# Block order of a two-layer SSM and SwiGLU kernel: the second layer's block 0 taken third instead of fourth

## Chip, core and metric

The kernel runs on one core of a Trainium2 chip. The metric is device time in microseconds (us) of one execution. Before the change the median of three runs is 1167.27 us (1165.26 to 1168.05).

## What is computed

The input is a sequence of 2048 rows (time) by 512 columns (channels), float32. Two layers follow each other, with the same weights; each is an SSM part and an FFN part, both on the layer-normed input and with the input added back:

```
x = x + A(layernorm(x)); x = x + B(layernorm(x)); x = x + A(layernorm(x)); x = x + B(layernorm(x))
A: K = Re(sum_n C exp(dt A l) dt B)   # a filter of 2048 taps per channel, from 128 states
   y = irfft(rfft(u padded) * rfft(K padded))[:2048] + u * Dskip
B: (silu(x @ w_gate) * (x @ w_up)) @ w_down      # 512 -> 1376 -> 512
```

A is a causal convolution along the sequence. B works on each row alone.

## The kernel before

**Blocks.** The sequence is cut into NB = 4 blocks of T = 512 rows. A pair (l, b) names layer l and block b; (l, b) has an SSM block and an FFN block, eight pairs in all. SEQ (line 45) is the order in which they are taken. The first some 320 us of the kernel build the filter's spectra and split the weights into high and low float16 halves; then the eight pairs follow.

**SSM block** (`inputs`, `forward`, `ssm`, `ssm_half`). For each pair not prepared early, `inputs` (line 709) loads 512 rows (tile `n`, from the program's input in layer 0, from `xdr` in layer 1), normalises them (`norm_x`: row statistics on ACT, the power on POOL, L226 on DVE, L249 on ACT), and `forward` makes eight *steps*, one for each column half h and frequency part q. A step's forward transform is DVE work (bt, z, the low half of z, all L230) and 12 matmuls (L282, tile `pf`), copied by ACT to `u`, which POOL stores in `udr`. `ssm_half` then multiplies spectra on DVE: block b needs b + 1 products (L778) and b sums (L781) of 128x1024 a step, since it convolves with all earlier blocks of its layer, whose `u` and filter parts it loads over SP's queue (`uu`, `w`). So a step of block 0 has one such large operation, block 1 three, block 2 five, block 3 seven. L783 and L784 combine, the result is split in two (`yl`), 12 matmuls (L798, tile `pi`) transform back, and `combine` adds up (`bb`). After four steps some 14 DVE operations of 128x256 (L813 to L830, and L230 under `t1`, `t2`, `xf`, `xg`) add the half into `xt`. `ahead` holds inputs made one step before their use: the last step of a block already makes the first input of the next.

**FFN block** (`ffn`, `ffn_norm`). It works on two halves of 256 rows. `ffn_norm` takes row statistics on ACT, splits the normed rows into two float16 tiles (`nn`, on DVE L864) and transposes them by DMA over SP's queue into `mix`. Then come six groups of matmuls into `pgu`: five of 48 (L911, L912, L914) and a *remainder* of 48 small ones (L878 to L880) that stands first in its half; after each group ACT takes silu (L917), DVE multiplies (L918), ACT and DVE split (L919, L920). The down projection `py` (L926 to L928) is 66 matmuls of 512 columns, after each 33 of which DVE adds the residual (L931) and SP stores the rows to `xdr` (layer 0) or to the output. The last L931 of an FFN block marks its end.

**Dependences.** SSM block (0, b) reads the program's input and earlier blocks of its layer. SSM block (1, b) reads the output of FFN block (0, b) and the spectra of earlier blocks of layer 1. An FFN block reads its own SSM block.

**Order.** The loop at the end of the kernel writes the SSM block of the pair i + 1 and then the FFN block of the pair i. From there on a list scheduler places instructions on each engine's queue by priorities: FFN evacuations and norms and the transform matmuls are high, the rest goes by the place in the program. On the chip each engine works through its queue in that fixed order. Tiles come from pools with few buffers (`n` 1, `u` 2, `w` and `uu` 3), and `xs` rotates over three blocks by the index in SEQ. HALF and INV (both 2) say from which index in SEQ the transforms use float16 halves; they are indices, so the third pair is the first of that kind under both orders.

Of the kernel before, what the change touches and what calls it, by code (L numbers as in the profile page):

```python
# [41 lines left out]
HALF = 2  # L42
INV = 2
LOW = [a for a in range(1, 33) if a % 2] + [8, 16, 24, 32]
SEQ = ((0, 0), (0, 1), (0, 2), (1, 0), (0, 3), (1, 1), (1, 2), (1, 3))


def dft_constants():
# [26 lines left out]
def kernel(ctx, tc, x, a_re, a_im, b_re, b_im, c_re, c_im, log_dt, d_skip,  # L75
# [12 lines left out]
    def tl(shape, name, tag, dt=F32):  # L88
        return sb.tile(shape, dt, name=name, tag=tag, bufs=BUFS[tag])
# [4 lines left out]
    def psml(shape, name):  # L94
        return ps.tile(shape, F32, name=name, tag="sml", bufs=4)
# [133 lines left out]
    def stt(o, i0, s, i1, op1):  # L229
        V.scalar_tensor_tensor(o, i0, s, i1, OP.mult, op1)  # L230

    def load_x(xt, layer, b):
        if layer == 0:
            nc.sync.dma_start(xt, x[0, b * T:(b + 1) * T, :].rearrange("(c p) d -> p c d", p=P))
        else:
            nc.sync.dma_start(xt, xdr[b].rearrange("c p d -> p c d"))
# [5 lines left out]
    def whole(t):  # L242

        return t.rearrange("p i (c d) -> p i c d", c=NQ)

    def norm_x(n):
        rs, nb = row_stats(n, 4, 1.0, "stats", lambda r: tl([P, D], "junk", "t1", BF16))
        for c in range(4):
            A.activation(n[:, c], n[:, c], AF.Identity, scale=rs[:, c:c + 1], bias=nb[:, c:c + 1])  # L249
# [454 lines left out]
    def inputs():  # L704

        for layer, b in SEQ:
            if layer == 0 and b < 2:
                if b == 0:
                    nc.sync.dma_start(u4, udr[0][0, 0].rearrange("q p c i d -> p q c i d"))
                for h in range(2):  # L710
                    for i, q in enumerate(QORD):
                        if b == 0:
                            u = u4[:, q]
                            for qn in (QORD[:3], QORD[3:], (), ())[i] if h else ():
                                nc.sync.dma_start(u4[:, qn], udr[0][0, 1, qn])
                        else:
                            u = tl([P, NQ, 2, DC], "u", "u")
                            nc.sync.dma_start(u, udr[0][b, h, q])
                        yield h, q, u
                continue  # L720
            n = tl([P, 4, D], "n", "n")
            load_x(n, layer, b)
            norm_x(n)
            if (layer, b) == SEQ[HALF]:
                eh.append(tl([P, 4, 3, 2, P], "eh", "ef", F16))
                nc.sync.dma_start(eh[0], c_eh)
            for h in range(2):
                for q, u in forward(n, h, eh[0] if eh else None):
                    if b < NB - 1:
                        G.dma_start(udr[layer][b, h, q], u)  # L730
                    yield h, q, u

    def ssm(layer, b):

        if (layer, b) == SEQ[INV]:
            nc.sync.dma_start(eih, c_eih)
        for h in range(2):
            yield from ssm_half(layer, b, h)

    def ssm_half(layer, b, h):  # L740
        first = layer == 0 and b == 0
        half = SEQ.index((layer, b)) >= INV
        hs = slice(h * HD, (h + 1) * HD)
        bb = {}

        def combine(q, pi):
            if q < 2:
                pair = tl([P, 2, 2, HD], "bb", "bd") if h == 0 or not first else bb1[:, q]
                bb[q], bb[q, 1] = pair[:, 0], pair[:, 1]
                A.activation(bb[q], pi, AF.Copy, scale=sy[:, 1:2] if half else 1.0)  # L750
                return
            s = bb[3 - q]
            bb[q] = bb[3 - q, 1]
            if half:
                stt(bb[q], pi, sy[:, 2:3], s, OP.add)
                stt(s, pi, sy[:, 1:2], s, OP.add)
            else:
                V.tensor_tensor(bb[q], s, pi, OP.subtract)
                V.tensor_tensor(s, s, pi, OP.add)

        late = []
        for _ in range(4):
            hq, q, u = ahead.pop(0)
            nxt = next(spec, None)
            if nxt:
                ahead.append(nxt)
            yk = tl([P, NQ, 2, 2, DC], "yk", "y1")
            y = yc if half else tl([P, 2, HD], "yf", "w")
            for k in range(b + 1):
                if k == 0:  # L770
                    w, uu = w0r[:, h, q], u
                else:
                    w = tl([P, NQ, 2, DC], "w", "w")
                    nc.sync.dma_start(w, wdr[k, h, q])
                    uu = tl([P, NQ, 2, DC], "uu", "uu")
                    nc.sync.dma_start(uu, udr[layer][b - k, h, q])
                t = tl([P, NQ, 2, 2, DC], "t", "t") if k else yk
                V.tensor_tensor(t, uu.unsqueeze(2).to_broadcast([P, NQ, 2, 2, DC]),  # L778
                                w.unsqueeze(3).to_broadcast([P, NQ, 2, 2, DC]), OP.mult)
                if k:  # L780
                    V.tensor_tensor(yk, yk, t, OP.add)  # L781
            yo = whole(y)
            V.tensor_tensor(yo[:, 0], yk[:, :, 0, 0], yk[:, :, 1, 1], OP.subtract)  # L783
            V.tensor_tensor(yo[:, 1], yk[:, :, 0, 1], yk[:, :, 1, 0], OP.add)  # L784
            if half:
                yl = yl2[:, QORD.index(q) % 2]
                A.activation(yl[:, 0], y, AF.Copy, scale=sy[:, 0:1])
                stt(yl[:, 1], y, sy[:, 0:1], yl[:, 0], OP.subtract)
            pi = psml([P, 2, HD], "pi")
            with tc.high_priority(offset=0 if first else BOOST):  # L790
                for o in range(2):
                    if half:
                        terms = [(eih[:, q, 0 if i == o else 1 + o, le], yl[:, ly, i])
                                 for i in range(2) for le, ly in ((0, 0), (0, 1), (1, 0))]
                    else:
                        terms = [(ei[:, q, 0 if i == o else 1 + o], y[:, i]) for i in range(2)]
                    for k, (e, m) in enumerate(terms):
                        PE.matmul(pi[:, o], lhsT=e, rhs=m, start=k == 0, stop=k == len(terms) - 1)  # L798
            late.append((q, pi))
            if first and q < 2 or len(late) > 1:  # L800
                combine(*late.pop(-1 if first and q < 2 else 0))
            yield
        for l in late:
            combine(*l)
        s03, e03, d03, f03 = bb[0][:, 0], bb[0][:, 1], bb[3][:, 0], bb[3][:, 1]
        s12, e12, d12, f12 = bb[1][:, 0], bb[1][:, 1], bb[2][:, 0], bb[2][:, 1]
        xt = xs[SEQ.index((layer, b)) % 3]
        if h == 0 and not first:
            load_x(xt, layer, b)
        o = [xt[:, c, hs] for c in range(4)]  # L810
        t1 = tl([P, HD], "t1", "t1")
        t2 = tl([P, HD], "t2", "t1")
        V.tensor_tensor(t1, s03, s12, OP.add)  # L813
        stt(t2, d12, TT, e12, OP.subtract)
        V.tensor_tensor(o[0], o[0], t1, OP.add)
        stt(t1, e03, -TT, d03, OP.add)
        V.tensor_tensor(t1, t1, t2, OP.add)
        stt(o[1], t1, CC, o[1], OP.add)
        yield
        t1 = tl([P, HD], "t1", "t1")  # L820
        t2 = tl([P, HD], "t2", "t1")
        V.tensor_tensor(s03, s03, s12, OP.subtract)
        V.tensor_tensor(f03, f03, f12, OP.add)
        stt(t2, d03, TT, e03, OP.subtract)
        stt(t1, e12, TT, d12, OP.subtract)
        V.tensor_tensor(s03, s03, f03, OP.subtract)
        V.tensor_tensor(t1, t1, t2, OP.add)
        stt(o[2], s03, HH, o[2], OP.add)
        stt(o[3], t1, CC, o[3], OP.add)
        yield  # L830
# [22 lines left out]
    def ffn_norm(layer, b, s):  # L853

        rows = TB // P
        xt = xs[SEQ.index((layer, b)) % 3][:, s * rows:(s + 1) * rows]
        nh, nlo = nhl2[:, s % 2, 0], nhl2[:, s % 2, 1]
# [95 lines left out]
    with tc.manual_schedule(engines={mybir.EngineType.Activation, mybir.EngineType.DVE, mybir.EngineType.PE, mybir.EngineType.Pool}):  # L953
# [167 lines left out]
        spec, ahead = inputs(), []  # L1121
# [27 lines left out]
        load_x(xs[0], 0, 0)  # L1149
        split(0, 0, 3)  # L1150
        conv = [ssm_half(0, 0, h) for h in range(2)]

        def slots():
# [115 lines left out]
```

## Time and profile before

| | |
|---|---|
| median of three runs | 1167.27 us |
| profiled execution, its own time | 1163.83 us |
| its span, first to last instruction | 1161.1 us |
| mean granted TensorE clock | 0.989 |
| PE busy (weight loads) | 95% (76%) |
| DVE, ACT, POOL busy | 86%, 52%, 9% |
| 9942 matmuls, 1586 DVE instructions | |

PE is TensorE's matmuls and PEld its weight loads, which run beside them; DVE is VectorE, ACT ScalarE, POOL GpSimd, SP the queue that issues most DMAs. A busy share is of the span. Matmuls overlap in the pipeline, so the duration of one is longer than the distance between two starts. In a row of the timeline stand start and duration in us, engine, line, operation, output and input by the program's names, the count, and in brackets the idle time before it and who ended it. All times are of the one profiled execution.

### The profile page before, as it was taken

What the parts mean: (1) busy time and instruction counts of PE and PEld (TensorE: products, weight loads), DVE (VectorE), ACT (ScalarE), POOL (GpSimd) and SP (SyncE); (2) the same over time, 40 slices, a digit from 0 to 9 for tenths busy, and PEclk for the clock granted to TensorE, in tenths of its full rate; (3) what the DMA queues carried; (4) which work ended last, traced back from release to release, by engine and by line L of the source; (5) the groups of instructions that cost most, each with busy time, mean ns of one, the idle gap of its engine ahead of it and who ended that gap; (6) DMA issues with size and microseconds to landing.
All of it is one profiled execution on the core that took longest, in us unless ns stands there. A gap on an engine that the chain in (4) does not pass through costs nothing.

```text
span 1161.1 us, 24400 instructions
## 1 busy us (share of the span) xinstructions
PE 1101.9 (95%) x9942; PEld 877.3 (76%) x9942; DVE 998.6 (86%) x1586; ACT 599.7 (52%) x1198; POOL 109.7 (9%) x162
## 2 busy tenths in 40 slices
PE   2989999998889999999999999999999999999998
PEld 1868888886776868687868687868777686876875
DVE  7999999968789999999899999989994999983212
ACT  6889898733553463557453533655433452334211
POOL 1112222210000010010010000210000010000000
PEclk9989999998899999999999999999999999999999
DMA  5357677866394437332264444343534145312000
GB/s 208 129 162 164 161 178 175 187 172 226 112 289 119 145 119 222 105 111 74 79 155 134 127 161 145 103 132 88 164 109 150 49 121 158 102 42 46 15 23 19
DMA packets 127314, 150.38 MB, mean 130 GB/s; under 512 B 50897, under 2 KB 75985, under 8 KB 127202
## 3 DMA queue, kind: packets, MB, share of 16 engines
q1 hardware_dynamic: 115298, 123.32, 34.9%
q0 software_dynamic: 11904, 25.50, 9.5%
q8 instruction: 78, 1.28, 0.5%
q14 instruction: 34, 0.28, 0.1%
HBM read 98.70 MB, written 33.82 MB: 114 GB/s over the span
## 4 chain that ended last, share of the span: by engine, by line
DVE 30%; PE 30%; issue 7%; DMA 4%; ACT 3%; SPq 1%; POOL 1%; DVEq 0%; ACTq 0%; POOLq 0%
PE pgu L911 5%; PE pgu L912 5%; PE pgu L914 5%; DVE t L778 5%; DVE yk L781 4%; PE py L926 3%; PE py L927 3%; PE py L928 3%; DVE yk L778 3%; DVE z L230 3%; DVE sg L918 2%; PE pi L798 2%; PE pf L282 2%; DVE hl L920 2%; DMA w<-wdr 2%
## 5 line engine op out<-in xcount | busy, mean ns | idle before, releaser
L911 PE MATMUL pgu<-mix,wsl 128*128 128x256 f16 x1280 | 299.2, 273 | 5.5 <-DVE sg L918 5.0
L912 PE MATMUL pgu<-mix,wsl 128*128 128x256 f16 x1280 | 298.9, 273 | 0.0
L914 PE MATMUL pgu<-mix,wsl 128*128 128x256 f16 x1280 | 195.2, 273 | 0.0
L912 PEld LDWEIGHTS <-wsl 128*128 128x128 f16 x1280 | 125.2, 98 | 22.7 <-issue 6.4
L926 PE MATMUL py<-wsl,hh 128*128 128x512 f16 (+1 forms) x352 | 133.5, 379 | 4.9 <-DVE xg L931 3.0
L911 PEld LDWEIGHTS <-wsl 128*128 128x128 f16 x1280 | 125.1, 98 | 16.4
L914 PEld LDWEIGHTS <-wsl 128*128 128x128 f16 x1280 | 125.2, 98 | 15.3
L928 PE MATMUL py<-wsl,hl 128*128 128x512 f16 (+1 forms) x352 | 133.4, 379 | 0.5 <-DVE hl L920 0.5
L927 PE MATMUL py<-wsl,hh 128*128 128x512 f16 x320 | 121.3, 379 | 0.0
L778 DVE TENSOR_TENSOR t<-uu,w 128x1024 f32<-128x1024 f32 x96 | 116.9, 1218 | 3.5 <-DMA w<-wdr 3.2
L917 ACT ACTIVATE sg<-pgu,sc 128x512 f32<-128x512 f32 x80 | 54.6, 683 | 125.1 <-PE pgu L914 121.8
L781 DVE TENSOR_TENSOR yk<-yk,t 128x1024 f32<-128x1024 f32 x96 | 116.8, 1217 | 0.2
L918 DVE SCALAR_TENSOR_TENSOR sg<-pgu,sc,sg 128x512 f32<-128x512 f32 x80 | 59.6, 745 | 52.1 <-ACT sg L917 51.9
L533 PE MATMUL pw<-kt,ek 128*128 128x256 f32 (+1 forms) x384 | 92.2, 378 | 0.0
L919 ACT ACTIVATE hh<-sg 128x512 f16<-128x512 f32 x80 | 50.1, 627 | 79.5 <-DVE sg L918 79.5
L533 PEld LDWEIGHTS pw<-kt,ek 128*128 128x128 f32 x384 | 73.6, 196 | 8.6
L798 PE MATMUL pi<-yl,mix 128*128 128x256 f16 x576 | 78.9, 273 | 0.6 <-DVE yl L230 0.3
L282 PE MATMUL pf<-z,eh 128*128 128x256 f16 x576 | 74.9, 273 | 0.6 <-DVE z L230 0.6
L778 DVE TENSOR_TENSOR yk<-u,w0r 128x1024 f32<-128x1024 f32 x56 | 68.1, 1217 | 0.8 <-ACT u L284 0.8
L498 PE MATMUL pk<-re,g 128*32 128x64 f32 x1024 | 65.1, 317 | 3.6 <-DMA g<-g 1.9
L920 DVE TENSOR_TENSOR hl<-sg,hh 128x512 f16<-128x512 f32 x80 | 54.9, 686 | 15.5 <-ACT hh L919 15.4
L927 PEld LDWEIGHTS <-hh 128*128 128x128 f16 (+1 forms) x352 | 34.4, 98 | 41.6 <-issue 6.0
(237 smaller groups left out, 2165.9 us busy)
## 6 DMA issues: line engine op xcount, KB each, us to landing
w<-wdr SPq DMA_DIRECT2D x96, 256.0 KB, 2.7
uu<-udr SPq DMA_DIRECT2D x96, 256.0 KB, 3.0
udr<-u POOLq DMA_DIRECT2D x32, 256.0 KB, 2.6
g<-g POOLq DMA_DIRECT2D x6, 1024.0 KB, 9.1
udr<-u SPq DMA_DIRECT2D x16, 256.0 KB, 3.0
n<-xdr SPq DMA_DIRECT2D x4, 1024.0 KB, 5.7
kdr<-ks SPq DMA_DIRECT2D x6, 512.0 KB, 2.6
kt<-kdr SPq DMA_DIRECT2D x24, 128.0 KB, 2.9
```

What stands on the lines that cost most here:

```text
L282: PE.matmul(pf[:, o], lhsT=e, rhs=m, start=k == 0, stop=k == len(terms) - 1)
L533: PE.matmul(pw[:, i], lhsT=e, rhs=kt[:, :, c + 4 * k0:4 * k1:4, :].rearrange("p g k d -> p k g d"), start=c == 0, stop=c == 3)
L778: V.tensor_tensor(t, uu.unsqueeze(2).to_broadcast([P, NQ, 2, 2, DC]), w.unsqueeze(3).to_broadcast([P, NQ, 2, 2, DC]), OP.mult)
L781: V.tensor_tensor(yk, yk, t, OP.add)
L798: PE.matmul(pi[:, o], lhsT=e, rhs=m, start=k == 0, stop=k == len(terms) - 1)
L911: PE.matmul(o, lhsT=wgu(wi, k, 0)[:, fs], rhs=nh[:, k], start=k == 0, stop=False)
L912: PE.matmul(o, lhsT=wgu(wi, k, 1)[:, fs], rhs=nh[:, k], start=False, stop=False)
L914: PE.matmul(o, lhsT=wgu(wi, k, 0)[:, fs], rhs=nlo[:, k], start=False, stop=k == 3)
L918: V.scalar_tensor_tensor(sg, pgu[:, 1], sc6[:, 4:5], sg, OP.mult, OP.mult)
L926: PE.matmul(py[:, r], lhsT=hh[:n, f, rc], rhs=wd(f, 0)[:n], start=f == 0, stop=False)
L927: PE.matmul(py[:, r], lhsT=hh[:n, f, rc], rhs=wd(f, 1)[:n], start=False, stop=False)
L928: PE.matmul(py[:, r], lhsT=hl[:n, f, rc], rhs=wd(f, 0)[:n], start=False, stop=f == FT - 1)
```

## The change

Two entries of SEQ change places, so that (1, 0) is taken third and (0, 2) fourth. FFN block (0, 0), on which SSM block (1, 0) depends, is written after SSM block (0, 1); so the early input of the third pair can no longer be made in the last step of SSM block (0, 1), and the second part of the diff leaves it out there (nxt is None at that one step) and makes it at the first step of the third pair.

```diff
-SEQ = ((0, 0), (0, 1), (0, 2), (1, 0), (0, 3), (1, 1), (1, 2), (1, 3))
+SEQ = ((0, 0), (0, 1), (1, 0), (0, 2), (0, 3), (1, 1), (1, 2), (1, 3))
...
         late = []
-        for _ in range(4):
+        for s in range(4):
+            if not ahead:
+                ahead.append(next(spec))
             hq, q, u = ahead.pop(0)
-            nxt = next(spec, None)
+            nxt = None if (layer, b, h, s) == (*SEQ[1], 1, 3) else next(spec, None)
             if nxt:
                 ahead.append(nxt)
```

Lines behind line 762 have numbers that are higher by two in the changed kernel (L778 is L780 there, L918 L920, L920 L922, L931 L933, L864 L866).

The queues change at these places. The first is DVE in the second half of FFN block (0, 0). Before the change, from that half's fourth group (L918) on; the products are those of the first two steps of SSM block (0, 2), bt is its forward transform:

```order
L918 SCALAR_TENSOR_TENSOR sg_3072<-pgu,sc_92,sg_3072 128x512
L783 TENSOR_TENSOR mix<-yk 128x256
L784 TENSOR_TENSOR mix<-yk 128x256
L778 TENSOR_TENSOR t<-uu,w 128x1024
L230 SCALAR_TENSOR_TENSOR xg<-t_3318,xg 128x256
L230 SCALAR_TENSOR_TENSOR t_3326<-bb 128x256
L629 TENSOR_SCALAR sy<-sy 128x1
L230 SCALAR_TENSOR_TENSOR bt<-n 128x256 x6
L778 TENSOR_TENSOR yk<-u,w0r 128x1024
```

With the change, from the third group on (the nn splits are those of FFN block (0, 1)):

```order
L920 SCALAR_TENSOR_TENSOR sg_3072<-pgu,sc_92,sg_3072 128x512
L866 TENSOR_TENSOR nn_3036<-nn_3036 128x512
L922 TENSOR_TENSOR hl<-sg_3072,hh 128x512
L866 TENSOR_TENSOR nn_3036<-nn_3036 128x512
L920 SCALAR_TENSOR_TENSOR sg_3072<-pgu,sc_92,sg_3072 128x512
L922 TENSOR_TENSOR hl<-sg_3072,hh 128x512
L226 SCALAR_TENSOR_TENSOR rs<-mv,rs 128x2
L920 SCALAR_TENSOR_TENSOR sg_3072<-pgu,sc_92,sg_3072 128x512
```

The products and transforms of SSM block (0, 2) have left the place; FFN operations and the norms of the next FFN block are what is left. The first forward operation of SSM block (1, 0) (bt) stands behind the fourth group of FFN block (0, 1).

The second place is DVE behind the last residual add of FFN block (0, 1). Before the change (the add, L931, is the first row; bt and z are those of SSM block (0, 3), L918 is FFN block (0, 2)'s second group):

```order
L931 SCALAR_TENSOR_TENSOR xg<-py,sc_92,xg 128x512
L230 SCALAR_TENSOR_TENSOR bt<-n 128x256 x4
L230 SCALAR_TENSOR_TENSOR z_3073<-bt 128x256 x2
L230 SCALAR_TENSOR_TENSOR z_3073<-z_3073 128x2x256
L230 SCALAR_TENSOR_TENSOR z_3073<-bt 128x256 x2
L918 SCALAR_TENSOR_TENSOR sg_3072<-pgu,sc_92,sg_3072 128x512
```

With the change 15 instructions stand between that add and the first of these rows, which end with the second nn split of the next FFN block, (1, 0); `xf` is the block's `xt`, and the products (L780, L783) are those of the second and third step of SSM block (0, 2):

```order
L780 TENSOR_TENSOR t_5484<-uu_5482,w_5480 128x1024
L230 SCALAR_TENSOR_TENSOR xf_3075<-t1_4558,xf_3075 128x256
L226 SCALAR_TENSOR_TENSOR rs_5918<-mv_5917,rs_5918 128x2
L783 TENSOR_TENSOR yk_5471<-yk_5471,t_5484 128x1024
L785 TENSOR_TENSOR mix_2445<-yk_5471 128x256
L786 TENSOR_TENSOR mix_2445<-yk_5471 128x256
L780 TENSOR_TENSOR t_5532<-uu_5530,w_5528 128x1024
L866 TENSOR_TENSOR nn2_3036<-nn2_3036 128x512
L780 TENSOR_TENSOR yk_5526<-u_5468,w0r_91 128x1024
L230 SCALAR_TENSOR_TENSOR yl2_3074<-mix_2445,sy_94,yl2_3074 128x512
L783 TENSOR_TENSOR yk_5526<-yk_5526,t_5532 128x1024
L866 TENSOR_TENSOR nn2_3036<-nn2_3036 128x512
```

The norm of the next FFN block stood well ahead of that add before; now it stands 27 instructions behind it. Behind the last residual add of FFN block (0, 2) the changed queue reads in the same way, with 32 instructions up to the second nn split of FFN block (0, 3).

## Prediction

> **What bounds the kernel now.** I read the kernel by stages first: one window for each of the eight FFN blocks, cut where the last residual add of a block (L931) starts on DVE. Columns: stretch, its length, busy time (and count) of PE, PE's weight loads, DVE, ACT, POOL, then the granted clock, DMA share, GB/s.
>
> ```profile
> 340.00:440.00 100.00, 97.90 (x788) 73.42 (x787) 96.48 (x166) 44.96 (x90) 8.87 (x11) 1.00 0.46 134
> 440.00:559.00 119.00, 117.35 (x1002) 92.29 (x1000) 114.28 (x210) 68.00 (x137) 11.91 (x18) 1.00 0.38 120
> 559.00:666.00 107.00, 105.19 (x890) 81.42 (x888) 103.70 (x165) 47.96 (x94) 6.29 (x5) 1.00 0.47 131
> 666.00:776.00 110.00, 109.40 (x930) 85.39 (x929) 107.35 (x184) 56.39 (x109) 11.72 (x13) 1.00 0.42 128
> 776.00:881.00 105.00, 104.23 (x884) 80.86 (x883) 102.05 (x162) 43.17 (x79) 7.03 (x12) 1.00 0.43 130
> 881.00:979.00 98.00, 97.44 (x821) 74.69 (x820) 80.40 (x128) 44.62 (x90) 6.36 (x5) 1.00 0.40 114
> 979.00:1075.00 96.00, 95.65 (x807) 73.25 (x805) 69.40 (x109) 33.01 (x61) 1.80 (x4) 1.00 0.24 70
> 1075.00:1161.00 86.00, 81.28 (x644) 59.89 (x641) 18.22 (x26) 13.95 (x22) 0.20 (x1) 0.99 0.06 19
> ```
>
> From 440 on PE never rests: between 440 and 1075 its idle time is 1.7 + 1.8 + 0.6 + 0.8 + 0.6 + 0.3 = 5.8 us. DVE is as full until 881 and then empties. So the end is PE's amount of work plus the time in which PE has nothing ready. The change moves work and takes none away; it can gain at most those 5.8 us and loses each microsecond in which PE starves. PE is fed because the next FFN block's input is ready early:
>
> ```profile
> 520.47 0.15 DVE L226 SCALAR_TENSOR_TENSOR rs<-mv,rs 128x2 f32<-128x2 f32 x1
> 558.04 0.75 DVE L931 SCALAR_TENSOR_TENSOR xg<-py,sc,xg 128x512 f32<-128x512 f32 x1
> ```
>
> At 520 the normalisation of FFN block (0,2) has its scale; the add that ends FFN block (0,1) comes at 558. The stock is over 30 us. The question is whether it survives.
>
> **What the change does to the stock.** SSM block (1,0) now stands third, and its input is the output of FFN block (0,0). While PE does that FFN, DVE, which in the old order worked on SSM block (0,2), has only FFN operations. The trace shows what such a dependence costs, since SSM block (1,3) waits for FFN block (0,3):
>
> ```profile
> 438.28 0.74 DVE L931 SCALAR_TENSOR_TENSOR xg<-py,sc,xg 128x512 f32<-128x512 f32 x1
> ...
> 879.59 0.75 DVE L931 SCALAR_TENSOR_TENSOR xg<-py,sc,xg 128x512 f32<-128x512 f32 x1
> ...
> 901.60 2.14 DVE L230 SCALAR_TENSOR_TENSOR bt<-n 128x256 f32<-128x256 f32 x6 [1.42 <-ACT n L249]
> ...
> 1106.84 0.75 DVE L931 SCALAR_TENSOR_TENSOR xg<-py,sc,xg 128x512 f32<-128x512 f32 x1 [4.50 <-PE py L928]
> ...
> 1149.04 0.75 DVE L931 SCALAR_TENSOR_TENSOR xg<-py,sc,xg 128x512 f32<-128x512 f32 x1 [4.21 <-PE py L928]
> ```
>
> From the add to the first forward operation (bt) pass 22.0 us: store, load, row statistics on ACT. Two adds of successive half blocks, with PE alone at work, are 42.2 us apart: an FFN half is 42.2 us of PE, a block 84.4. The matmuls of the transforms come from the chain of waits, the DVE prices from the groups (last numbers: busy us, mean ns):
>
> ```profile
> 437.39 1.31 PE pf L282 x12
> ```
> ```profile
> L778 DVE TENSOR_TENSOR t<-uu,w 128x1024 f32<-128x1024 f32 x96 | 116.9, 1218 | 3.5 <-DMA w<-wdr 3.2
> L781 DVE TENSOR_TENSOR yk<-yk,t 128x1024 f32<-128x1024 f32 x96 | 116.8, 1217 | 0.2
> L230 DVE SCALAR_TENSOR_TENSOR z<-bt 128x256 f32<-128x256 f32 x96 | 36.3, 417 | 0.1
> L230 DVE SCALAR_TENSOR_TENSOR bb<-pi,sy,bb 128x512 f32<-128x512 f32 x48 | 35.7, 744 | 4.3 <-PE pi L798 4.2
> L864 DVE TENSOR_TENSOR nn<-nn 128x512 f16<-128x512 f32 x30 | 20.5, 684 | 6.1 <-ACT nn L863 3.1 <-DMA mix<-nn 3.1
> L918 DVE SCALAR_TENSOR_TENSOR sg<-pgu,sc,sg 128x512 f32<-128x512 f32 x80 | 59.6, 745 | 52.1 <-ACT sg L917 51.9
> L920 DVE TENSOR_TENSOR hl<-sg,hh 128x512 f16<-128x512 f32 x80 | 54.9, 686 | 15.5 <-ACT hh L919 15.4
> ```
> ```profile
> 434.06 0.42 DVE L783 TENSOR_TENSOR mix<-yk 128x256 f32<-128x256 f32 x1
> 434.41 0.42 DVE L784 TENSOR_TENSOR mix<-yk 128x256 f32<-128x256 f32 x1
> 434.74 1.22 DVE L778 TENSOR_TENSOR t<-uu,w 128x1024 f32<-128x1024 f32 x1
> ```
>
> So a transform matmul is 0.109 us (1.31 / 12). DVE instructions in a row start 0.07 us before the last has ended (0.34 us apart at 0.42 us each), so I count 1.15 for the large ones, 0.345 for 128x256, 0.67 and 0.61 for the middle ones.
>
> **Start.** In front of the add at 438.3 PE no longer does six transforms of SSM block (0,2), 72 matmuls or 7.9 us; so FFN block (0,0) ends at 430.9 (13 small matmuls moved in front of it are 0.5). SSM block (1,0) starts at 430.9 + 22.0 = 452.9 on DVE. PE has five FFN groups to do until then and loses under 1 us (I take 0.8).
>
> **First border, FFN (0,1) to (1,0).** PE has 84.4 - 2 (a remainder already done) + 216 x 0.109 = 106.0 us from 430.9, so it ends FFN block (0,1) at 537.7. In its order the last inverse transform of SSM block (1,0) stands 42 matmuls of 512 columns and 12 of 256 ahead of that end, 10.4 us: 527.3. From there DVE has 54 instructions up to and with the second nn split (L864 before, L866 after) that FFN block (1,0) needs: 12 large (13.8), 30 of 128x256 (10.4), 5 splits (3.1), 6 middle ones (4.0): 31.3 us, so that this split starts at 558.0 and the next instruction at 558.6. The way from split to matmul is this one:
>
> ```profile
> 424.78 0.68 DVE L864 TENSOR_TENSOR nn<-nn 128x512 f16<-128x512 f32 x1
> ```
> ```profile
> 429.04 0.22 PE L880 MATMUL pgu<-wsl,mix 128*128 128x96 f16 x1 [0.37 <-DMA mix<-nn]
> ```
>
> 4.3 us through ACT's share and two transposing DMAs: PE goes on at 562.2. In between it has 48 transform matmuls and half a remainder, 6.4 us. **Stall: 562.2 - 537.7 - 6.4 = 18.1 us.** No such wait stands in the trace; its bounds are 0 (the stock is there, as at 520) and 24.5 (PE finds nothing else).
>
> **Second border, (1,0) to (0,2).** From 562.2 PE needs 101.6 us to the end of FFN block (1,0), and 1.7 for the clock (below): 665.5. From 558.6 DVE needs 102.5 us to the end of the split for the next block; with the 4.3 us from the split's start that is 664.8. It holds by 0.7 us; I take no stall. A measured tie of this kind does not stand in the trace: bounds 0 and the 5 us that DVE would lose at 5%.
>
> **Third border, (0,2) to (0,3).** PE: two blocks 168.8, less 1.1 done, and 360 transform matmuls 39.2: 206.9 from 562.2, and the 1.7: FFN block (0,2) ends at 770.8. DVE: 375 instructions up to the split: 98 large (112.7), 152 of 128x256 (52.4), 64 at 0.67 (42.9), 47 at 0.61 (28.7), 14 small (3.3), 240 us from 558.6, since SSM blocks (0,2) and (0,3), the two costly convolutions of the first layer, now follow each other. The split's own 0.6 goes off, so it starts at 798.0 (a wait of 1.4 as before the row at 901.60 could come on top; I leave it to the range). PE goes on at 802.3, with 9.3 us of its own in between, and border waits such as those of 559 to 666 (1.8) run beside. **Stall: 802.3 - 770.8 - 1.8 - 9.3 = 20.4 us**; bounds 0 and 31.5. After that SSM block (1,1), with three large DVE operations per step in place of the seven of (0,3), refills the stock, and the wait of (1,3) is covered by DVE's queue.
>
> **Clock.** A stall of PE is followed by half speed:
>
> ```profile
> 333.50:336.80 3.30, 3.03 (x15) 0.51 0.97 196
> ```
> ```profile
> 333.77 0.37 PE L911 MATMUL pgu<-mix,wsl 128*128 128x256 f16 x1 [4.59 <-DVE sg L918]
> ```
>
> After 4.6 us without work the granted clock is 0.51 for 3.3 us: 1.7 us lost, 3.4 for two stalls.
>
> **Sum.** 18.1 + 20.4 + 0.8 + 3.4 = 42.7, less the small waits of 440 to 776 that the stalls swallow (1.7 + 1.8 + 0.6 = 4.1): 38.6 us on the span of 1161.1, or 1202.4 for the profiled execution, which took 1163.8. That is 3.4 below the median of 1167.3 of the runs shown; on the median I forecast **1206 us**.
>
> A rule against this sum: the Trainium skill (Perfetto Trace Analysis, Identifying the Most-Contended Engine) says that matmul busy time is not a good measure of how near TensorE is to its limit, and that the busy share of weight loads is better. By it PE would have 22% of the window 440 to 559 to spare (92.29 of 119), more than all stalls, and the time would stay at 1167. The trace disagrees: in the last window PE's loads are busy 70% with DVE nearly idle, and the half block still takes 42.2 us.
>
> **Rivals.**
> - Only the first stall (chance 0.17): DVE's order at the third border lets the split through early, or PE's own work covers it. 18.1 + 0.8 + 1.7 - 4.1 = 16.5: 1184 us. For it: the borders hang on differences of a few us between sums of 200.
> - More than forecast (0.20): DVE loses 5% between 558 and 798, 12 us; 5 show at the second border, where the margin is 1, the rest at the third. The wait for FFN block (0,0) can grow too if SP's queue holds the load behind transposes. 38.6 + 12 + 3 for the load: 1221 us.
> - No change (0.05): the FFN inputs are ready at each border as at 520, since the block now third is the cheapest (one product per frequency part): 1167 us. Against it: the DVE order shows FFN operations alone where SSM work stood.
> - PE has room to spare, as a kernel whose matmul pipeline is not full (0.02): PE would make up the 38.6 us in the blocks that follow: 1167 us. Against it: the 42.2 us. The page of the Trainium skill named above would have it so.
> - Faster (0.02): the 22.0 us wait of DVE at 880 disappears under queued work. It decides if PE later waits for SSM block (1,3); PE idles 0.9 us between 881 and 1075, so with all 5.8 us of idle time gone it would be 1161 us.
>
> **The numbers.** Forecast (1206) 0.54, with a range of its own of 1193 to 1216. The range for 8 in 10 takes in the first rival and most of the second: 1182 to 1224. The measurement tells about 0.3% (3.5 us) from no change. Faster 0.02, same 0.07, slower 0.91.
>
> **What would show it.** In the changed profile PE should stand idle some 18 us near 540 to 562 and 20 us near 775 to 800, released by transposing DMAs, with DVE without a gap there and idle between about 410 and 450; PE's busy time should be unchanged, and the FFN blocks from (1,1) on without stalls. A PE without gaps at these borders would prove me wrong; so would gaps of another place, above all inside SSM block (1,0) between 453 and 527.

## The result and the profile after

The changed kernel takes 1207.9 us (median of four runs, 1207.53 to 1210.2), the kernel before 1166.55 us on the same chip (1165.26 to 1168.05). The ratio is 1.037 with a 95% interval of 1.0352 to 1.0388: slower, by 41.4 us by the medians alone (their quotient is 1.035). The profiled execution took 1210.2 us, with a span of 1208.2, so it lies 2.3 above its median; by spans the change costs 1208.2 - 1161.1 = 47.1 us.

First the first lines of the two pages: engine, busy us, share of the span, instructions. Before:

```profile
PE 1101.9 (95%) x9942; PEld 877.3 (76%) x9942; DVE 998.6 (86%) x1586; ACT 599.7 (52%) x1198; POOL 109.7 (9%) x162
```

After:

```profile
PE 1115.8 (92%) x9942; PEld 883.4 (73%) x9942; DVE 1001.3 (83%) x1586; ACT 600.7 (50%) x1198; POOL 107.8 (9%) x162
```

The counts are equal. PE's idle time grew from 59.2 us (1161.1 - 1101.9) to 92.4 (1208.2 - 1115.8), so by 33.2; PE's busy time grew by 13.9 for the same matmuls. That is half speed: from 340 on, in windows of 1 us, the granted clock is near 0.5 for some 37 us, PE is busy 26 of them, and half of that, 13, is nearly the whole growth; before the change no such window stands up to the last matmul. The two amounts make up the 47.1.

Next the stages, with the two borders as windows of their own (columns as in the prediction: length, busy PE, weight loads, DVE, ACT, POOL, granted clock, DMA share, GB/s).

```profile
340.00:430.00 90.00, 88.37 (x703) 65.80 (x702) 61.58 (x110) 26.50 (x52) 2.01 (x5) 1.00 0.35 99
430.00:541.00 111.00, 107.70 (x878) 83.19 (x876) 78.22 (x152) 53.33 (x106) 8.61 (x14) 1.00 0.23 79
541.00:560.00 19.00, 8.17 (x42) 5.32 (x40) 15.62 (x27) 8.36 (x15) 4.24 (x3) 0.58 0.91 249
560.00:671.00 111.00, 107.73 (x901) 83.41 (x902) 109.28 (x176) 54.18 (x108) 8.79 (x10) 0.98 0.42 125
671.00:785.00 114.00, 109.33 (x899) 83.47 (x898) 110.95 (x170) 45.02 (x83) 4.33 (x8) 0.99 0.44 126
785.00:802.00 17.00, 8.06 (x44) 5.49 (x44) 17.00 (x31) 10.17 (x18) 1.84 (x3) 0.73 0.76 249
802.00:920.00 118.00, 114.87 (x988) 90.11 (x986) 106.82 (x182) 59.12 (x118) 11.32 (x14) 0.98 0.40 106
920.00:1028.00 108.00, 105.40 (x890) 81.57 (x888) 104.08 (x166) 49.57 (x98) 8.56 (x7) 1.00 0.45 135
1028.00:1121.00 93.00, 92.20 (x772) 70.07 (x771) 71.23 (x111) 33.15 (x61) 2.37 (x4) 1.00 0.29 74
1121.00:1208.00 87.00, 82.37 (x654) 61.02 (x651) 18.26 (x27) 13.96 (x22) 0.20 (x1) 1.00 0.06 19
```

Before, DVE was nearly full from 340 on. Now it is idle first (28.4 + 32.8 us in the first two rows) and full afterwards, and PE, which was idle only 5.8 us between 440 and 1075, stands still 10.8 us in the third row and 8.9 in the sixth, and some microseconds in each block from 560 to 1028. The timeline of DVE shows why it is idle: the last add of FFN block (0, 0), and the first forward operation of SSM block (1, 0).

```profile
429.11 0.75 DVE L933 SCALAR_TENSOR_TENSOR xg<-py,sc,xg 128x512 f32<-128x512 f32 x1 [5.46 <-PE py L930]
451.60 2.14 DVE L230 SCALAR_TENSOR_TENSOR bt<-n 128x256 f32<-128x256 f32 x6 [1.42 <-ACT n L249]
```

22.5 us lie between them. What follows at the first border is in PE's timeline: the last down projection of FFN block (0, 1), the waits, and the first matmul (L882) that goes on with FFN block (1, 0).

```profile
537.33 0.38 PE L930 MATMUL py<-wsl,hl 96*128 96x512 f16 x1
539.54 0.27 PE L800 MATMUL pi<-yl,mix 128*128 128x256 f16 x1 [1.83 <-ACT yl L789]
...
545.06 2.50 PE L800 MATMUL pi<-yl,mix 128*128 128x256 f16 x11 [3.06 <-DVE yl L230]
553.41 0.37 PE L800 MATMUL pi<-yl,mix 128*128 128x256 f16 x1 [5.84 <-ACT yl L789]
...
560.02 0.22 PE L882 MATMUL pgu<-wsl,mix 128*128 128x96 f16 x1 [1.95 <-DMA mix<-nn]
```

Four waits, 12.7 us. Only the last, 1.95 us, is for the input of the FFN block and is ended by a transposing DMA. The other three stand in front of transforms of SSM block (0, 2) that come first in PE's queue; ACT and DVE are named for them, but ACT's yl waits for DVE's products. The third border, FFN (0, 2) to (0, 3), reads in the same way:

```profile
780.72 0.38 PE L930 MATMUL py<-wsl,hl 96*128 96x512 f16 x1
...
787.61 0.27 PE L800 MATMUL pi<-yl,mix 128*128 128x256 f16 x1 [3.33 <-ACT yl L789]
...
789.26 2.51 PE L282 MATMUL pf<-z,eh 128*128 128x256 f16 x11 [1.27 <-DVE z L230]
...
796.95 0.37 PE L800 MATMUL pi<-yl,mix 128*128 128x256 f16 x1 [3.44 <-ACT yl L789]
...
801.67 0.26 PE L882 MATMUL pgu<-wsl,mix 128*128 128x96 f16 x1 [1.62 <-DMA mix<-nn]
```

### The profile page after: what moved, and what is told of

The parts are those of the page before. It is cut to its first block, busy times and chain, and to the rows that moved or that the text cites. A ratio compares the mean times of both kernels' runs of the same rounds, so it can differ in the third digit from the quotient of the medians.

```text
span 1208.2 us, 24394 instructions
## 1 busy us (share of the span) xinstructions
PE 1115.8 (92%) x9942; PEld 883.4 (73%) x9942; DVE 1001.3 (83%) x1586; ACT 600.7 (50%) x1198; POOL 107.8 (9%) x162
## 4 chain that ended last, share of the span: by engine, by line
PE 37%; DVE 20%; issue 8%; DMA 5%; ACT 4%; POOL 1%; SPq 1%; DVEq 0%; POOLq 0%; ACTq 0%
PE pgu L913 6%; PE pgu L914 6%; PE pgu L916 6%; PE py L928 3%; PE py L930 3%; DVE t L780 3%; PE py L929 3%; PE pi L800 3%; PE pf L282 3%; DVE yk L783 3%; DMA mix<-nn 2%; DVE yk L780 2%; DVE z L230 2%; POOL rs L225 1%; DVE sg L920 1%
## 5 line engine op out<-in xcount | busy, mean ns | idle before, releaser
L780 DVE TENSOR_TENSOR t<-uu,w 128x1024 f32<-128x1024 f32 x96 | 116.8, 1216 | 3.7 <-DMA w<-wdr 3.4
L783 DVE TENSOR_TENSOR yk<-yk,t 128x1024 f32<-128x1024 f32 x96 | 116.6, 1215 | 0.3
L920 DVE SCALAR_TENSOR_TENSOR sg<-pgu,sc,sg 128x512 f32<-128x512 f32 x80 | 59.5, 744 | 57.2 <-ACT sg L919 57.0
L800 PE MATMUL pi<-yl,mix 128*128 128x256 f16 x576 | 81.8, 280 | 21.7 <-ACT yl L789 17.8
L282 PEld LDWEIGHTS <-eh 128*128 128x128 f16 x576 | 58.0, 101 | 31.7 <-issue 21.8
L282 PE MATMUL pf<-z,eh 128*128 128x256 f16 x576 | 79.0, 284 | 2.2 <-DVE z L230 2.2
L780 DVE TENSOR_TENSOR yk<-u,w0r 128x1024 f32<-128x1024 f32 x56 | 68.1, 1217 | 11.1 <-ACT u L284 10.9
L929 PEld LDWEIGHTS <-hh 128*128 128x128 f16 (+1 forms) x352 | 34.6, 98 | 48.4 <-issue 12.6
```

Of the source, the lines that this page charges most:

```text
L282: PE.matmul(pf[:, o], lhsT=e, rhs=m, start=k == 0, stop=k == len(terms) - 1)
L920: V.scalar_tensor_tensor(sg, pgu[:, 1], sc6[:, 4:5], sg, OP.mult, OP.mult)
L929: PE.matmul(py[:, r], lhsT=hh[:n, f, rc], rhs=wd(f, 1)[:n], start=False, stop=False)
```

## The experiments

**Theories.** Theory 1: the wait of SSM block (1, 0) takes work from DVE, and since DVE and PE are nearly balanced up to the end of the first layer, DVE's lost time comes back as PE's lost time. Theory 2: what counts is the place of a few operations in DVE's queue at the borders. Theory 3: the two costly SSM blocks (0, 2) and (0, 3) side by side are the trouble. Theory 4: the second part of the diff, the late input, makes the loss. In the lists below "loss" is the median of a kernel less the median of the kernel before in the runs on the same chip; the change itself has 41.4.

### The wait made longer and shorter

```diff
+                if (layer, b) == (1, 0):          # double_wait
+                    G.dma_start(xd2, n)
+                    G.dma_start(n, xd2)
...
-            load_x(n, layer, b)                   # direct_norm
-            norm_x(n)
+            src = xs[0] if (layer, b) == (1, 0) else n
+            if src is n:
+                load_x(n, layer, b)
+            norm_x(n, src)
```

In direct_norm `norm_x` has a second argument, the tile that it reads.

> The changed kernel, in which the input of SSM block (1,0), once loaded, is stored to another place in DRAM and loaded again before it is normalised, on POOL's queue: a longer wait with no new work for PE, DVE or ACT. A store and a load took some 10 us of the 22 in the changed kernel. Theory 1 (each microsecond that DVE loses while PE does FFN block (0,0) is lost for the end): slower by 8 to 14 us, 1216 to 1222. Theory 2 (only places in the queues count, and they stay): 1206 to 1211 us.

> The changed kernel, in which the normalisation of SSM block (1,0) reads the output of FFN block (0,0) where it lies in SBUF, and not after a store to DRAM and a load. That takes the store and the load, some 10 us, out of the 22 us between the last add of FFN block (0,0) and the first operation of (1,0) on DVE. Theory 1 (DVE's lost time is never made up until the end of the layer): DVE starts 8 to 10 us earlier and the time falls by 4 to 10 us, to 1198 to 1204. Theory 2 (order of the queue at the border): the last inverse transform of (1,0) stands at the same place of PE's order, so the stall stays, 1205 to 1210 us.

Measured: 1220.06 us with the longer wait (ratio 1.0461, 1.0429 to 1.0493; loss 55.2) and 1193.08 with the shorter one (1.0249, 1.0233 to 1.0266; loss 28.8). The wait itself stands in DVE's timeline, the last add of FFN block (0, 0) and the first bt of (1, 0). Shorter:

```profile
427.56 0.75 DVE L935 SCALAR_TENSOR_TENSOR xg<-py,sc,xg 128x512 f32<-128x512 f32 x1 [5.46 <-PE py L932]
435.79 2.13 DVE L230 SCALAR_TENSOR_TENSOR bt<-n 128x256 f32<-128x256 f32 x6 [1.52 <-ACT n L249]
```

Longer:

```profile
429.66 0.75 DVE L937 SCALAR_TENSOR_TENSOR xg<-py,sc,xg 128x512 f32<-128x512 f32 x1 [5.46 <-PE py L934]
...
465.80 2.14 DVE L231 SCALAR_TENSOR_TENSOR bt<-n 128x256 f32<-128x256 f32 x6 [2.29 <-ACT n L250]
```

The waits are 8.2, 22.5 and 36.1 us, the losses 28.8, 41.4 and 55.2. So 14.3 us of wait less give 12.6 us, and 13.6 us more cost 13.8: nearly one for one on both sides, as far as losses that are known to 2 to 4 us can tell. The longer wait lies in the range of theory 1. The shorter one lies below both ranges: it gained more than I had written because it also lets ACT take the statistics of the first rows early, so the wait shrank by 14.3 and not by 10.

The places in the queue did not stay as they were, as the first expectation had it. The scheduler answers to each wait: between the add and bt stand one FFN multiplication (sg) with the shorter wait, three in the changed kernel and five with the longer one. So the runs price the wait together with the order that the scheduler makes for it; the wait alone, in an unchanged queue, was not measured.

### The wait taken away

```diff
-            load_x(n, layer, b)
+            load_x(n, 0 if b == 0 else layer, b)
```

> This kernel is the changed one, but SSM block (1,0) normalises the program's input x instead of the output of FFN block (0,0), so that part of the computation is changed; the amount and kind of work on every engine is the same, and only the wait is gone. Theory 1 (amount of work: DVE stands idle while (1,0) waits, some 38 us between 400 and 452, and what it does not do there is missing up to the end of the first layer): DVE has work in that stretch, the stall at 540 to 560 goes and the later small waits of PE go with it, so 1168 to 1178 us. Theory 2 (queue order: the final adds and the normalisation of the next FFN block stand behind products on DVE, whatever has gone before): the stalls at the borders stay about as they are, 1195 to 1208 us.

Measured: 1172.4 us, ratio 1.0071 (1.0056 to 1.0086), loss 8.1, in the range of theory 1. The first bt now comes 29.9 us before the last add of FFN block (0, 0), which is at 438.80:

```profile
408.92 2.14 DVE L230 SCALAR_TENSOR_TENSOR bt<-n 128x256 f32<-128x256 f32 x6 [1.43 <-ACT n L249]
```

DVE's busy time between 380 and 528, one row each, shows what the wait does; without it, the changed kernel, and the longer wait:

```profile
380.00:528.00 148.00, 147.02 (x1237) 117.04 (x1236) 121.66 (x239) 83.50 (x171) 12.48 (x20) 1.00 0.35 107
```

```profile
380.00:528.00 148.00, 147.18 (x1216) 114.82 (x1215) 89.51 (x177) 68.72 (x137) 9.67 (x16) 1.00 0.25 79
```

```profile
380.00:528.00 148.00, 144.85 (x1192) 112.58 (x1191) 84.11 (x164) 64.16 (x129) 9.68 (x17) 1.00 0.29 93
```

PE is as full in the second row as in the first; only DVE has 32 us less done. The loss is 33 us higher (41.4 - 8.1), and it appears from 538 on, 86 us after the end of the wait that causes it. So of the loss some 33 us belong to the dependence, with the order that the scheduler makes for it, and 8 stay when it is gone; 3 of these stand between 340 and 400, where PE is busy 55.80 us against 58.81 before the change. DVE's work in this stretch gives the direction of the loss and not its exact size: the shorter wait has 104.56 us there, so the steps from one run to the next are 17.1, 15.1 and 5.4 us of DVE's work, and the losses grow by 20.7, 12.6 and 13.8.

### The same wait where it is covered

```diff
+            src = xs[1] if (layer, b) == (1, 3) else n     # in the kernel before
+            if src is n:
+                load_x(n, layer, b)
+            norm_x(n, src)
```

> The kernel before, in which the normalisation of SSM block (1,3) reads the output of FFN block (0,3) in SBUF, without the store and the load: the wait of 22 us at 880 us, which leaves DVE without work for 15 us, becomes some 10 us shorter. If a wait of this kind counts only where DVE's work is needed later than PE can cover it (theory 1: behind it stand cheap blocks, and PE is never without work), 1162 to 1168 us. If DVE's wait were lost time at any place, 1154 to 1158 us.

Measured: 1167.25 us, ratio 1.0022 (1.0007 to 1.0036), loss 2.4: no gain, rather a trace of a loss. From the add to bt:

```profile
877.73 0.75 DVE L933 SCALAR_TENSOR_TENSOR xg<-py,sc,xg 128x512 f32<-128x512 f32 x1
886.01 2.14 DVE L230 SCALAR_TENSOR_TENSOR bt<-n 128x256 f32<-128x256 f32 x6 [1.56 <-ACT n L249]
```

The wait fell from 22.0 to 8.3 us and nothing came of it. The same wait counts in full in front of the costly blocks of the first layer, and nothing at the end of it, where DVE has little left to do.

### The late input and the order, each alone

```diff
-SEQ = ((0, 0), (0, 1), (1, 0), (0, 2), (0, 3), (1, 1), (1, 2), (1, 3))
+SEQ = ((0, 0), (0, 1), (0, 2), (1, 0), (0, 3), (1, 1), (1, 2), (1, 3))   # late_only, rest as changed
...
-            nxt = None if (layer, b, h, s) == (*SEQ[1], 1, 3) else next(spec, None)
+            nxt = next(spec, None)                                           # cut_early, with the cut above
...
+SEQ = ((0, 0), (0, 1), (0, 2), (0, 3), (1, 0), (1, 1), (1, 2), (1, 3))   # layer_order, rest as before
```

> The order of blocks is that of the kernel before; only the second part of the diff stays: the spectrum of the third block's first pair is made when that block asks for it, and not during the last step of the block ahead. Theories 1 and 2 both put the loss on the order of blocks: 1165 to 1171 us. Theory 4 (the late input of the third pair makes the loss): 1185 us or more. If this part costs something small, 2 to 6 us, that amount is no part of the loss by the order.

> The order of blocks is that of the changed kernel, but SSM block (1,0) normalises the program's input x in place of the output of FFN block (0,0), so that part of the computation is changed; and its first pair is made during the last step of SSM block (0,1), as the third block's was in the kernel before. The order alone is left, with neither the wait for FFN block (0,0) nor the late input. Theory 1 (only DVE's idle time while PE does FFN block (0,0) is lost): DVE has work there as in the kernel before, 1162 to 1168 us. Theory 3 (the neighbourhood of the two costly SSM blocks (0,2) and (0,3) makes a loss of its own at the third border): 1172 us or more.

> The kernel before, with the blocks taken layer by layer: (0,2) and (0,3) are neighbours as in the changed kernel, and (1,0) comes fifth, with its input long ready. Theory 1: DVE has the same work and no wait in the first layer, so PE stays fed until FFN block (0,3) or nearly so; with less cheap work between, a few microseconds at most, 1162 to 1175 us. Theory 3 (two costly SSM blocks side by side empty the stock by themselves): 1180 us or more, with a stall of PE at the border of FFN blocks (0,2) and (0,3).

Measured: late_only 1175.39 (1.0097, 1.008 to 1.0114; loss 11.1), cut_early 1177.27 (1.0102, 1.007 to 1.0133; loss 11.5), layer_order 1176.97 (1.0099, 1.0082 to 1.0116; loss 11.2). I had written under 1171 for the first and under 1168 for the second, and both are wrong; layer_order lies between its two ranges. In late_only part of the cause can be read: the block's first forward work waits, and DVE is idle while PE is full. The stretch 400 to 420 in late_only, and before the change:

```profile
400.00:420.00 20.00, 20.00 (x154) 14.77 (x153) 10.36 (x22) 15.74 (x33) 2.16 (x3) 1.00 0.14 27
```

```profile
400.00:420.00 20.00, 20.00 (x171) 16.47 (x169) 20.00 (x42) 11.93 (x24) 4.00 (x4) 1.00 0.28 93
```

DVE loses 9.6 us there in the way of theory 1, without any dependence on an FFN block. Theory 4 as I had put it (1185 or more) falls, but the late input is not free. In cut_early a part of the dependence was left: the residual input of (1, 0) still comes from `xdr`, and DVE stops for it.

```profile
453.94 0.42 DVE L817 TENSOR_TENSOR xf<-xf,t 128x256 f32<-128x256 f32 x1 [3.11 <-DMA xf<-xdr]
```

DVE is idle 13.7 us between 440 and 480 there. So the run does not stand for the order alone, as I had meant it to. Its time lies in the range of theory 3, but neither it nor layer_order shows what theory 3 says: no stall stands at the border of (0, 2) and (0, 3), and the largest wait of PE in cut_early between 400 and 1040 is in another place:

```profile
656.54 0.38 PE L928 MATMUL py<-wsl,hh 128*128 128x512 f16 x1 [2.70 <-DVE xf L933]
```

The rest are waits of at most 1.5 us; together PE waits 15.4 us in that stretch, in layer_order 15.5, in late_only 16.6, before the change 6.6. The losses do not add up either: cut_dep has the order and the late input and loses 8.1. By spans layer_order loses 15.1 us (1176.2 - 1161.1): 8.9 are these waits, and PE is at half speed for some 10 us near 552 and 717. Why the order of before has so few of these waits stays open.

### Less work for DVE

```diff
-            for k in range(b + 1):
+            for k in range(1 if (layer, b) == (0, 2) else b + 1):          # after_less, before_less
+            for k in range(1 if (layer, b, h) == (0, 2, 0) else b + 1):    # less_early; less_late with h = 1
```

> The changed kernel without the products of SSM block (0,2) with the two older blocks: 32 large DVE operations (16 multiplications and 16 additions, 37 us at 1.15 us each) and their loads are left out, between 450 and 680 us, so that block's convolution is not complete. Theory 1 (from 528 us on DVE's amount of work sets the pace and PE has room): the time falls by most of the loss, to 1168 to 1185 us, and the stall near 790 goes. Theory 2 (order of the queue at the borders, not the amount): the last inverse and the split keep their places, the time falls by less than 12 us, 1196 to 1208 us.

> The kernel before without the same 32 large DVE operations of SSM block (0,2), whose convolution is then not complete. Theory 1: with the old order PE is never without work, so the same 37 us of DVE buy nothing or at most the 5.8 us in which PE is idle between 440 and 1075: 1159 to 1167 us. If DVE paced the kernel before as well, it would be 1140 us or less.

> The changed kernel without the products of SSM block (0,2) with the two older blocks in the first half of the channels: 16 large DVE operations (18 us) and their loads are left out, most of them those that stand in DVE's queue between the last inverse of (1,0) and the split for FFN block (1,0), so that block's convolution is not complete. Theory 1 (amount): leaving out all 32 gave 12 us, so half gives about 6, 1199 to 1204 us, as in the run that leaves out the later half. Theory 2 (the products ahead of that split): nearly all of the 12 us come from here, 1194 to 1199 us.

> The same with the products of the second half of the channels in place of the first: 16 large DVE operations (18 us) fewer, all of them behind the first border's split, with that block's convolution not complete. Theory 1 (amount, wherever it falls before the third border): 1199 to 1204 us, as with the first half. Theory 2 (place): 1205 to 1209 us.

Measured: after_less 1195.58 (1.0255, 1.0223 to 1.0286; loss 29.8), less_early 1189.5 (1.0199, 1.0169 to 1.023; loss 24.7), less_late 1201.08 (1.0308, 1.0279 to 1.0336; loss 36.3), before_less 1173.2 (1.006, 1.004 to 1.008; loss 7.5). Against the loss of 41.4, the 18.4 us of the early half give 16.7, those of the late half 5.1, all 36.8 only 11.6; and in the kernel before less work costs 7.5, which neither range had. Here too the scheduler makes other queues in each run. Theory 1 in its plain form, an amount that counts wherever it falls, is wrong, and so is theory 2, which had nothing for the late half and less for the early one. Where work is left out early, PE finds its operands sooner at the first border; less_early:

```profile
546.71 1.47 PE L282 MATMUL pf<-z,eh 128*128 128x256 f16 x11 [2.87 <-DVE z L230]
...
550.12 2.51 PE L800 MATMUL pi<-yl,mix 128*128 128x256 f16 x11 [1.27 <-DVE yl L230]
...
555.56 0.22 PE L882 MATMUL pgu<-wsl,mix 128*128 128x96 f16 x1
```

There is no wait of 5.84 us and none at L882, and DVE's later waits stay small (2.2 us in all between 560 and 800). In less_late DVE comes to places of its queue where it must wait itself, 10.3 us between 560 and 800:

```profile
617.34 0.75 DVE L933 SCALAR_TENSOR_TENSOR xf<-py,sc,xf 128x512 f32<-128x512 f32 x1 [2.16 <-PE py L930]
620.07 0.75 DVE L230 SCALAR_TENSOR_TENSOR bb<-pi,sy,bb 128x512 f32<-128x512 f32 x1 [1.98 <-PE pi L800]
```

In each row DVE stands in front of an operation for which PE is not ready, and in the second the next product of the SSM block, which starts at 620.74, is queued behind it. The spared time is stood away there. In before_less the chain runs over three engines. ACT's row:

```profile
456.15 0.63 ACT L221 ACTIVATE junk<-n 128x512 bf16<-128x512 f32 x1 [5.46 <-DMA n<-xdr]
```

DVE's:

```profile
460.76 0.75 DVE L230 SCALAR_TENSOR_TENSOR yl<-mix,sy,yl 128x512 f16<-128x512 f32 x1 [7.94 <-ACT yl L787]
```

PE's:

```profile
464.12 0.27 PE L911 MATMUL pgu<-mix,wsl 128*128 128x256 f16 x1 [4.46 <-DVE sg L918]
```

ACT stands 5.5 us in front of the row statistics of SSM block (1, 0), whose load from `xdr` waits for FFN block (0, 0) (its last add is at 445.17). Behind them in ACT's queue is the yl that DVE needs, behind that in DVE's queue an FFN multiplication (sg) that PE needs. So with the cheaper SSM block (0, 2) in front, the engines come to the dependence of (1, 0) before it is met, in the old order too. The amount of DVE's work counts as far as the fixed queues let the engines use the time. That is what is left of theory 1.

### Final adds ahead of products

```diff
+        with tc.high_priority(offset=0 if first else BOOST):
+            ... the late combinations, the final adds, the mixing adds
```

> The changed kernel, in which the last combinations, the final adds and the mixing adds of every SSM block after the first are given the raised priority that the FFN operations have, so that DVE takes them ahead of products of the next SSM block. Theory 2 (queue order): the split that PE waits for at the first border comes up to 14 us earlier (12 large operations go behind it), the stalls at the borders shrink and stay away, 1188 to 1198 us. Theory 1 (amount of DVE's work): the stall at 540 to 560 shrinks, but the products that go behind are then missing later, small waits between 560 and 1030 grow by as much, and the time is 1203 to 1211 us.

Measured: 1208.32 us, ratio 1.0374 (1.0356 to 1.0391), loss 44.1. The run tells nothing of theory 2 at the first border, since the queue hardly changed there: from the first bb behind the last inverse to the second nn split stand 12 large products in DVE's timeline, as in the changed kernel. The adds hang on each other and the products still go between them. Whether an order that holds the products back would shorten the stall was not tried in another way; less_early, which leaves most of them out, is the nearest to it.

## Why the prediction was right, point by point

**Start: right.** FFN block (0, 0) was to end at 430.9 and ended with the add at 429.11; the wait was taken as 22.0 us and is 22.5; bt was to start at 452.9 and starts at 451.60. That PE loses only 0.8 us there holds too (51.18 us busy between 400 and 452).

**First border: place right, path and split between idle and slow wrong.** PE was to end FFN block (0, 1) at 537.7; its last matmul runs from 537.33 to 537.71. PE was to go on at 562.2, and does at 560.02. I had counted up to the second of the two nn splits, forecast for 558.0; it starts at 560.07, and PE went on off the first, 6.4 us after it where 4.3 were counted. DVE's timeline has the two here, with those of the third border:

```profile
553.65 0.69 DVE L866 TENSOR_TENSOR nn<-nn 128x512 f16<-128x512 f32 x1
...
560.07 0.69 DVE L866 TENSOR_TENSOR nn<-nn 128x512 f16<-128x512 f32 x1 [2.80 <-DMA mix<-nn]
...
797.87 0.68 DVE L866 TENSOR_TENSOR nn<-nn 128x512 f16<-128x512 f32 x1
...
802.00 0.68 DVE L866 TENSOR_TENSOR nn<-nn 128x512 f16<-128x512 f32 x1
```

The 22.3 us from end to start were forecast as 24.5, of them 18.1 idle and 6.4 work. In fact 12.7 are idle, and 9.6 go to the work, at half speed. I had taken the transforms as work that fills the stall; PE's queue makes it wait in front of them, and a transposing DMA ends only the last wait.

**Second border: the tie did not hold.** I took no stall by a margin of 0.7 us. There is none at the border itself, but PE waits 2.5 us inside the block,

```profile
660.80 0.38 PE L928 MATMUL py<-wsl,hh 128*128 128x512 f16 x1 [2.53 <-DVE xf L933]
```

and ends FFN block (1, 0) near 668 where 665.5 was forecast. PE and DVE run in lockstep from 560 on, and each small slip between them counts.

**Third border: resumption met by chance, stall mis-sized.** DVE's 375 instructions, 98 of them large, reach to the second split. It was forecast for 798.0 and starts at 802.00: DVE set out 2.1 us late (560.68 for 558.6) and took 241.9 us in place of 240. PE was to go on at 802.3, and does at 801.67, but off the first split at 797.87; it has work until 806.98, where the first matmul that needs the second stands. A split that was 4.0 us late and a path that needs only the first made up for each other. And PE came to the border at 781.1, not at 770.8, so of the 20.4 us only 10.1 stand there (the four waits above and one of 0.39). The other 10 had been paid before, in half speed and in waits of 6.6 us together, the largest at 660.80 and 720.69 (2.13). As long as DVE sets the pace, as I read it, the place of a wait is open and the sum is fixed: DVE is busy 265.85 us of the 274 from 528 to 802.

```profile
528.00:802.00 274.00, 243.64 (x1938) 183.20 (x1937) 265.85 (x427) 121.63 (x232) 19.74 (x24) 0.94 0.48 140
```

**Idle time in all: right in the sum, not in its terms.** 18.1 + 20.4 + 0.8 - 4.1 = 35.2 us more idle time was forecast; it is 33.2. At the two borders 12.7 and 10.1 of it stand; the other 10 were forecast for no place.

**Clock: the term that was mis-sized.** 3.4 us were forecast for two stalls. PE's busy time grew by 13.9. The sign named at the end of the forecast, PE's busy time unchanged, failed with it, and did not agree with the 3.4 either. How this comes about is shown in the last section.

**After the third border: partly wrong.** I had PE without a stall there. It waits 3.1, 2.6 and 0.8 us in the stages from 802 to 1121 (1.7 before in the three stages that follow 776, without the last block). The wait of SSM block (1, 3) is covered as forecast: DVE is busy 104.08 of the 108 us from 920 on. The gaps inside SSM block (1, 0) that would have proved the forecast wrong do not stand: PE is busy 147.18 of the 148 us from 380 to 528.

**Sum.** 38.6 us were forecast on the span of one execution: 35.2 idle and 3.4 slow. There were 47.1: 33.2 and 13.9. So on spans the forecast was 8.5 us short: the slow term was too small by 10.5 and the idle term too large by 2.0. That 1206 us on the median met 1207.9 so closely is partly luck: the profiled execution before lies 2.7 us below the median of 1166.55 and the one after 2.3 above its own, so that by the medians only 41.4 us are to be explained. What the sum did not know is that it had put the whole loss on the dependence, while about 8 us stay without it. The late input, for which I had a price only through the moved transforms, costs 11.1 us by itself.

**The rivals.** "More than forecast" had the mechanism of the second border right (a few microseconds show there), but DVE's loss of 5% is 3% (8.2 of 274). "Only the first stall", "no change" and "faster" have no support. "PE has room to spare" did not hold. The rule of the Trainium skill (Perfetto Trace Analysis, Identifying the Most-Contended Engine) that weight-load time shows TensorE's headroom would have let PE absorb the loss; PE's loads went from 76% to 73% busy, and the span grew by more than PE's idle time. The room of the one window named for this rival was 26.7 us (119 - 92.29), less than the two stalls of 38.5 together, and not more, as the forecast had it.

## What to carry to other kernels

When two engines are balanced, as here, a dependence that lets one of them stand idle can cost nearly its full length even where the other is busy at the time; the bill comes one or two stages later, in many small waits, and here its sum was forecast better than its places. Ask of each wait what the waiting engine has to do until the stage ends: 14 us off a wait of 22 were worth nothing in front of cheap blocks, and 12.6 us in front of costly ones. Look at the queue of each variant too: the scheduler moves other work when a dependence changes. Leaving work out helps only where the engine's fixed queue lets it go on; elsewhere it meets the next operation that is not ready.

## What the runs showed of the hardware

The granted clock does not wait for a long gap. In windows of 3.4 us over the first border of the changed kernel:

```profile
536.70:540.10 3.40, 1.56 (x11) 0.86 (x10) 3.40 (x9) 1.14 (x2) 0.00 (x0) 1.00 0.13 50
540.10:543.50 3.40, 1.90 (x10) 1.19 (x8) 3.40 (x10) 1.12 (x2) 0.54 (x1) 0.50 0.73 231
543.50:547.00 3.50, 1.94 (x10) 1.35 (x10) 3.50 (x6) 1.56 (x5) 0.00 (x0) 0.50 0.64 153
...
553.80:557.20 3.40, 3.40 (x19) 2.41 (x18) 3.40 (x4) 2.27 (x4) 0.00 (x0) 0.51 0.83 209
557.20:560.60 3.40, 1.45 (x21) 1.11 (x20) 0.60 (x2) 0.29 (x1) 0.58 (x1) 0.99 1.12 122
```

A window in which PE is busy 1.56 of 3.40 us is followed by half speed, though the longest wait in it is 1.83 us. Half speed then stays through windows with 1.90 and 1.94 us of matmuls, 17.1 us in all, and ends behind the first window that is full. Eleven transform matmuls that run in the stall (from 545.06) take 2.50 us, where eleven at full speed take 1.36 (from 781.71), and so stretch the stall that slows them. A longer wait can go unpunished: the 2.53 us that end at 660.80 fall into two windows, and the clock stays at 1.00.

```profile
656.10:659.60 3.50, 2.17 (x14) 1.12 (x12) 3.23 (x7) 1.41 (x4) 2.55 (x1) 1.00 0.09 19
659.60:663.00 3.40, 2.20 (x11) 1.02 (x11) 3.08 (x5) 1.93 (x3) 0.29 (x1) 1.00 0.62 220
```

The third border narrows it: a window with 1.83 us of matmuls in 3.41 (782.44 to 785.85) leaves the clock at 1.00, the one from 785.85 to 789.26 with 0.38 us is followed by 0.50, and at half speed 2.55 us in 3.41 (796.09 to 799.50) do not bring the full clock back.

The Trainium skill (TensorE: Matmul & The Clock Gate, HAM oscillation — how this bites in real kernels) puts the rule as no gaps of PE above some 3.4 us. The steps of 3.4 us agree with these rows; the gap does not, since here a window that was a little under half busy was enough.
